# x placed in the output ahead of time, and the last addition of the result made by accumulating stores

## The chip, the cores and the metric

The kernel runs on one core of one Trainium2 chip. The metric is the device time of one execution in microseconds (us). Three runs of the kernel before gave a median of 2445.79 us, from 2444.87 to 2446.43.

## What is computed

For 2048 tokens x of width 1024, all in float32:

```python
xn = _layernorm(x)                                # over the last axis
s  = _A_ref(xn, A_wqkv, A_wo)                     # linear attention, 32 heads, then times wo
h  = _silu(xn @ w1) * (xn @ w3)                   # 3584 wide
g  = _silu(h @ w2)
return x + s * g
```

The change touches the last line: how `x` comes into `x + s * g`.

## The kernel before

Every large product is made with one level of a seven-product scheme (`B11`, `T2`, `T3`, `T1`, `B21`, `T4`, `B22`), each of the seven as three passes over operands that were split into a high and a low part (`split`, L80 to 88; `mm3`, L89 to 93). The split is a cast on ScalarE (ACT, L83) and a subtraction on VectorE (DVE, L84). The program goes through these stages:

1. **Start.** 512 tokens (`xa`) and 512 others (`xb`) are loaded by SyncE's queue (SP), normalised, turned by TensorE (PE, L148) and split. The first four weight tiles (`w0k0_0`, `w0v0_0`, `w0k0_1`, `w0v0_1`, L286) come through the same SP queue, and the first products `ak`, `av` need one of them each. `prepare_rest` forms sums of the tokens on GpSimd (POOL, L190 to 193). The next weights (`wk0_0`, `wv0_0`, L263) go into the two buffers that `xa` leaves, so their loads wait until the last of `xa` has been turned.
2. **Keys, values, queries, gate and up products** for the two halves of the tokens. Intermediates go to memory.
3. **Attention's end** (`s`), which stores s into `s_d`.
4. **The w2 product** in five layers `B0` to `B4` (`layers`), each over the 8 groups of 256 tokens (`NG` = 8, `m` = 0 to 7). A layer loads its left operands (`rA11B` and six others, L890, from `h_d` and `hs_d`), splits them, makes seven products for each group and adds them into the accumulators `acc0` to `acc7`. The additions are by DVE out of PSUM (L846 to L871) and by POOL (L849 to 851).

In the last layer, `B4`, every finished quarter of a group (128 x 512) goes through `finish`: SP loads `ss` (a piece of s) and `xs` (a piece of x); ACT takes the SiLU of the accumulator (L926); DVE multiplies by `ss` (L927) and adds `xs` (L928); POOL issues the store into `out` (L929). That is 32 quarters.

The order of instructions on each engine is not the order of the text: a scheduler with a simulated timeline sets it from dependencies when the program is built. Each engine then works its own list in order. The order of the SP list is the order in which transfers enter SP's queue.

Of the kernel before, what the change touches and what calls it, by code (L numbers as in the profile page):

```python
# [12 lines left out]
ALU = mybir.AluOpType  # L13
# [3 lines left out]
P = 128  # L17
# [5 lines left out]
def tile_linear_attention_times_swiglu(  # L23
# [10 lines left out]
    nc = tc.nc  # L34
    x, out = x[0], out[0]
# [71 lines left out]
    def small(name):  # L107
        return pc.tile([P, C], F32, tag="c", name=name)
# [344 lines left out]
    def half(h):  # L453
# [40 lines left out]
        for pair in range(ND // 2):  # L494
            if h == 0 and pair < 2:
                run(m[2 * pair])
                run(m[2 * pair + 1])
            elif h and pair == 0:
                side_by_side(keys(pair, paired=True), values(pair, paired=True))
            else:  # L500
                run(keys(pair))
                run(values(pair))
            later.extend(uses[pair][2])
# [263 lines left out]
    GT = 2 * P  # L767
    NG = S // GT
# [130 lines left out]
    def hiddens(i, m):  # L899
        h_ = h_d[i][m // NT].rearrange("p (k e) s -> p k e s", e=2)  # L900
        hs = hs_d[i][m // NT]
        return left(m, m % NT, [h_[:, :, e] for e in range(2)], [hs[:, :, e] for e in range(2)],
                    (FB[i][1] - FB[i][0]) // 2, f"B{i}")

    def second_weights(i, n, k):
        t = small(f"r{n}B{i}_{k}")
        nc.sync.dma_start(out=t, in_=second_weight(i, n, k))
        return t
# [9 lines left out]
    def store_s(m, t, n, a):  # L918
        nc.gpsimd.dma_start(out=s_d[2 * m + t][:, n * C:(n + 1) * C], in_=a)  # L919

    def finish(m, t, n, a):
        r0, cols = (2 * m + t) * P, slice(n * C, (n + 1) * C)
        xs, ss = small(f"xs{m}_{t}{n}"), small(f"ss{m}_{t}{n}")
        nc.sync.dma_start(out=ss, in_=s_d[2 * m + t][:, cols])
        nc.sync.dma_start(out=xs, in_=x[r0:r0 + P, cols])
        nc.scalar.activation(a, a, AF.Silu)  # L926
        nc.vector.tensor_mul(a, a, ss)  # L927
        nc.vector.tensor_add(a, a, xs)  # L928
        nc.gpsimd.dma_start(out=out[r0:r0 + P, cols], in_=a)  # L929

    def run(seg, nxt=None, around=None):

        def between(k):
            if m == NG - 1 and nxt:
                if k == 0:
                    nxt.operands(0)
                    for e in range(seg.nk, nxt.nk):
                        nxt.right(e)
                if k < nxt.nk:
                    nxt.right(k)  # L940

        if not seg.X:
            seg.operands(0)
        for m in range(NG):
            if m + 1 < NG:
                seg.operands(m + 1)
            seg.tokens(m, m == 0 or m == NG - 1 and nxt is not None, between)


# [26 lines left out]
    def layer_place(n, i, k):  # L976
# [3 lines left out]
    layers = [Segment(f"B{i}", (f1 - f0) // 2, i == 0, layer_place, lambda n, _, k, i=i: second_weights(i, n, k),  # L980
                      lambda m, i=i: hiddens(i, m), lambda m, t, n: acc[m][:, t, n],
                      finish if i == len(FB) - 1 else None)
              for i, (f0, f1) in enumerate(FB)]
# [2 lines left out]
        layers[0].right(k)  # L986
    acc.extend(pw.tile([P, 2, 2, C], F32, tag=f"acc{m}", name=f"acc{m}") for m in range(NG))
    for i, seg in enumerate(layers):
        run(seg, layers[i + 1] if i + 1 < len(layers) else None)


# [21 lines left out]
```

## Time and profile before

| | before |
|---|---|
| median of three runs | 2445.79 us |
| the profiled execution | 2438.58 us |
| its span in the trace | 2436.8 us |
| mean granted clock of TensorE | 0.992 |
| TensorE busy | 2344.2 us, 96% |
| VectorE busy | 1810.3 us, 74% |
| ScalarE busy | 928.0 us, 38% |
| GpSimd busy | 723.7 us, 30% |
| traffic | 408.62 MB, 168 GB/s |

The profiled execution is one of the kernel's executions, 7.2 us under the median of the three. Busy shares are means over stages that differ: the rows of single stretches tell which engine a stage waits for. A granted clock of 1.00 is 2.4 GHz, and 0.50 is 1.2 GHz.

### The profile page before, as it was taken

Reading aid. Unit: us, or ns where it says so; the run is one execution under the profiler, and the core shown is the slowest. Engines: PE = TensorE matmul, PEld = TensorE weight load, DVE = VectorE, ACT = ScalarE, POOL = GpSimd, SP = SyncE. Lnnn points to the kernel's source line nnn. Section 1 sums busy time; section 2 is a strip of 40 time slices with the busy share of each in tenths; the row PEclk is TensorE's granted clock in tenths of the full one; section 3 lists DMA queues with packets and bytes.
Section 4 is the critical chain, followed back from the end, with each engine's and each line's share of the span. In section 5 each row is a group of like instructions: output and inputs, shape, how many; then the busy total and the mean of one; then the engine's idle time right before and its main releaser. Section 6 shows DMA issues by size and latency. Waiting matters only on the chain.

```text
span 2436.8 us, 30795 instructions
## 1 busy us (share of the span) xinstructions
PE 2344.2 (96%) x10544; PEld 1927.2 (79%) x10544; DVE 1810.3 (74%) x2688; ACT 928.0 (38%) x1663; POOL 723.7 (30%) x909
## 2 busy tenths in 40 slices
PE   6999989999999999999999999999899999999987
PEld 5788777778888888888778888888687887778776
DVE  8645788888887764657888887888655767776797
ACT  4434544332333233445433323333323434343443
POOL 3000021465554310000343543244330032323253
PEclk9999999999999999999999999999999999999999
DMA  4221555665555581124455556457776545454587
GB/s 139 70 69 45 172 168 171 220 212 196 184 203 178 184 290 35 52 83 144 163 192 180 191 191 207 136 187 243 242 234 194 152 130 157 120 163 116 169 288 240
DMA packets 375133, 408.62 MB, mean 168 GB/s; under 512 B 19840, under 2 KB 308608, under 8 KB 374976
## 3 DMA queue, kind: packets, MB, share of 16 engines
q1 hardware_dynamic: 348800, 319.35, 41.9%
q0 software_dynamic: 26176, 87.31, 9.5%
q8 instruction: 82, 1.34, 0.2%
q14 instruction: 75, 0.61, 0.1%
HBM read 268.96 MB, written 137.63 MB: 167 GB/s over the span
## 4 chain that ended last, share of the span: by engine, by line
PE 75%; DVE 11%; DMA 6%; issue 5%; ACT 1%; POOL 1%; SPq 0%; DVEq 0%; POOLq 0%; ACTq 0%
PE dB L93 1%; PE kv L442 1%; PE cB L91 1%; PE dB L91 1%; PE dB L92 1%; PE cB L93 1%; PE cB L92 1%; PE aB L93 1%; PE aB L91 1%; PE aB L92 1%; DMA wpr<-wp_d 1%; PE trk L409 1%; PE trv L409 1%; DMA rA11B<-h_d 1%; PE cs L93 1%
## 5 line engine op out<-in xcount | busy, mean ns | idle before, releaser
L511 POOL DMA_DIRECT2D pq_d<-pq x32 | 17.5, 548 | 501.2 <-DVE pq L403 461.6
L564 POOL DMA_DIRECT2D h_d<-sg x112 | 62.0, 553 | 331.1 <-DVE sg L563 320.6
L849 POOL TENSOR_TENSOR acc<-acc,uB 128x512 f32<-128x512 f32 x25 | 41.9, 1676 | 157.8 <-DVE uB L846 157.8
L546 POOL TENSOR_TENSOR qd<-qd 128x128 f32<-128x128 f32 x32 | 25.4, 795 | 129.1 <-DVE qd L696 121.1
L578 POOL TENSOR_TENSOR w<-w 128x256 f32<-128x256 f32 x28 | 26.4, 944 | 106.7 <-DMA w<-in_B_w 106.5
L826 POOL TENSOR_TENSOR acc<-acc,uB 128x512 f32<-128x512 f32 x7 | 10.9, 1560 | 149.3 <-ACT uB L818 149.3
L410 ACT ACTIVATE kvr<-trk 128x512 f32<-128x512 f32 x32 | 19.1, 597 | 88.0 <-PE trk L409 84.8
L550 POOL TENSOR_TENSOR hs<-sg,hs 128x256 f32<-128x256 f32 x56 | 51.9, 927 | 1.7
L547 POOL TENSOR_TENSOR hs<-hs,sg 128x256 f32<-128x256 f32 x56 | 46.5, 830 | 0.0
L919 POOL DMA_DIRECT2D s_d<-s x32 | 17.5, 546 | 92.9 <-DVE s L856 41.6
L546 POOL TENSOR_TENSOR hs<-sg,sg 128x256 f32<-128x256 f32 x56 | 42.1, 751 | 1.0
L91 PE MATMUL cB<-T,XA22B 128*128 128x512 f32 x87 | 35.0, 403 | 7.3 <-DVE acc L853 7.0
L549 POOL TENSOR_TENSOR hs<-sg 128x256 f32<-128x256 f32 x56 | 41.5, 740 | 0.0
L83 ACT CAST XS4B<-rS4B 128x384 fp32r<-128x384 f32 (+1 forms) x40 | 19.6, 490 | 54.0 <-PE cB L93 44.6
L851 POOL TENSOR_TENSOR acc<-acc,uB 128x512 f32<-128x512 f32 x25 | 40.0, 1600 | 0.0
L84 DVE TENSOR_TENSOR XS1B<-rS1B,XS1B 128x384 fp32r<-128x384 f32 (+1 forms) x40 | 36.4, 910 | 4.1 <-ACT XS1B L83 4.0
L867 DVE TENSOR_TENSOR acc<-cB,acc 128x512 f32<-128x512 f32 x25 | 17.2, 688 | 29.7 <-PE cB L93 29.7
L83 ACT CAST XS1B<-rS1B 128x384 fp32r<-128x384 f32 (+1 forms) x40 | 19.7, 493 | 48.5 <-PE cB L93 26.2
L926 ACT ACTIVATE acc<-acc 128x512 f32<-128x512 f32 x32 | 20.2, 632 | 46.3 <-DVE acc L856 14.1
L83 ACT CAST XA11B<-rA11B 128x384 fp32r<-128x384 f32 (+1 forms) x40 | 19.7, 493 | 44.9 <-PE dB L93 28.4
L83 ACT CAST XS3B<-rS3B 128x384 fp32r<-128x384 f32 (+1 forms) x40 | 19.7, 491 | 43.3 <-DMA rS3B<-hs_d 20.5
L91 PE MATMUL aB<-B,XA12B 128*128 128x512 f32 x87 | 34.1, 392 | 1.9 <-ACT uB L843 1.9
(5861 smaller groups left out, 8899.6 us busy)
## 6 DMA issues: line engine op xcount, KB each, us to landing
h_d<-sg POOLq DMA_DIRECT2D x112, 256.0 KB, 3.1
qs_d<-qd POOLq DMA_DIRECT2D x32, 512.0 KB, 4.1
hs_d<-hs POOLq DMA_DIRECT2D x60, 256.0 KB, 3.5
w<-in_B_w SPq DMA_DIRECT2D x56, 256.0 KB
wt_d<-w SPq DMA_DIRECT2D x28, 512.0 KB
hs_d<-hs SPq DMA_DIRECT2D x52, 256.0 KB
pq_d<-pq POOLq DMA_DIRECT2D x32, 256.0 KB, 3.0
pqd<-pq_d SPq DMA_DIRECT2D x16, 512.0 KB
```

Of the source, the lines that this page charges most:

```text
L83: nc.scalar.copy(out=hi, in_=src)
L91: nc.tensor.matmul(acc, lhsT=wh, rhs=ah, start=start, stop=False, skip_group_check=True)
L92: nc.tensor.matmul(acc, lhsT=wh, rhs=al, start=False, stop=False, skip_group_check=True)
L93: nc.tensor.matmul(acc, lhsT=wl, rhs=ah, start=False, stop=stop, skip_group_check=True)
L409: nc.tensor.transpose(p_[:, t * P:(t + 1) * P], src[:, t * P:(t + 1) * P], ident)
L546: nc.gpsimd.tensor_add(out=s1, in0=a21, in1=a22)
L547: nc.gpsimd.tensor_sub(out=s2, in0=s1, in1=a11)
L549: nc.gpsimd.tensor_sub(out=s3, in0=a11, in1=a21)
L550: nc.gpsimd.tensor_sub(out=s4, in0=a12, in1=s2)
L564: nc.gpsimd.dma_start(out=h_d[i][2 * h + c][:, 2 * k + n], in_=sg[n, c])
L849: G.tensor_add(out=c22, in0=c22, in1=u)
L851: G.tensor_add(out=c12, in0=c12, in1=u)
```

## The change

`finish` no longer loads `xs` and no longer adds it for the groups `m` = 0 to 6. In its place their store into `out` adds to what lies there (`accum_op=ALU.add`). So that x lies there, seven transfers from `x` straight to `out`, of 256 tokens (1 MB) each, are put on SP's queue (`lay_x`). They are written in layer `B1`, ahead of the products of each group. Group 7 stays as before.

```diff
+    ADDED = NG - 1
+
     def finish(m, t, n, a):
         r0, cols = (2 * m + t) * P, slice(n * C, (n + 1) * C)
-        xs, ss = small(f"xs{m}_{t}{n}"), small(f"ss{m}_{t}{n}")
+        ss = small(f"ss{m}_{t}{n}")
         nc.sync.dma_start(out=ss, in_=s_d[2 * m + t][:, cols])
-        nc.sync.dma_start(out=xs, in_=x[r0:r0 + P, cols])
+        if m >= ADDED:
+            xs = small(f"xs{m}_{t}{n}")
+            nc.sync.dma_start(out=xs, in_=x[r0:r0 + P, cols])
         nc.scalar.activation(a, a, AF.Silu)
         nc.vector.tensor_mul(a, a, ss)
-        nc.vector.tensor_add(a, a, xs)
-        nc.gpsimd.dma_start(out=out[r0:r0 + P, cols], in_=a)
+        if m >= ADDED:
+            nc.vector.tensor_add(a, a, xs)
+            nc.gpsimd.dma_start(out=out[r0:r0 + P, cols], in_=a)
+        else:
+            nc.gpsimd.dma_start(out=out[r0:r0 + P, cols], in_=a, accum_op=ALU.add)
+
+    def lay_x(m):
+
+        if m < ADDED:
+            nc.sync.dma_start(out=out[m * GT:(m + 1) * GT, :], in_=x[m * GT:(m + 1) * GT, :])
...
         for m in range(NG):
             if m + 1 < NG:
                 seg.operands(m + 1)
+            if around:
+                around(m)
             seg.tokens(m, m == 0 or m == NG - 1 and nxt is not None, between)
...
-        run(seg, layers[i + 1] if i + 1 < len(layers) else None)
+        run(seg, layers[i + 1] if i + 1 < len(layers) else None, lay_x if i == 1 else None)
```

What the built programs do with it, at three places:

**SP's queue, at the very start of the program** (names: `w0v0_0` and `w0k0_1` are first weight tiles, `out_0` the output, `in_A_x` x):

```order
 L174 DMA xb1_426<-in_A_x 128x1024
 L174 DMA xb2_456<-in_A_x 128x1024
+L942 DMA out_0<-in_A_x 16x16384 x7
 L286 DMA w0v0_0__355<-in_A_wqkv 128x8x128
 L286 DMA w0k0_1__378<-in_A_wqkv 128x8x128
```

The seven transfers wait for no data, and the scheduler has placed all of them here, before the second weight tile and some 2000 us ahead of layer `B1`.

**DVE, the same stretch of the start, as it stands in the changed program** (`xb` are the second 512 tokens; the L84 rows with `w0v0_0`, `w0k0_1` and `w0v0_1` split the weight tiles; `xb3` is the last of the tokens):

```order
L141 TENSOR_SCALAR xb0_424<-xb0_424,mom_213 128x1024
L141 TENSOR_SCALAR xb1_426<-xb1_426,mom_213 128x1024
L403 SCALAR_TENSOR_TENSOR pk0_0_0_500,z_501<-ak0_0__341,pk0_0_0_500 128x512
L421 SCALAR_TENSOR_TENSOR zacc_74<-z_501,zacc_74 128x1
L84 TENSOR_TENSOR B11v0_0__357<-w0v0_0__355,B11v0_0__357 128x512
L84 TENSOR_TENSOR B21v0_0__360<-w0v0_0__355,B21v0_0__360 128x512
L84 TENSOR_TENSOR B11k0_1__380<-w0k0_1__378,B11k0_1__380 128x512
L84 TENSOR_TENSOR B21k0_1__383<-w0k0_1__378,B21k0_1__383 128x512
L84 TENSOR_TENSOR B11v0_1__403<-w0v0_1__401,B11v0_1__403 128x512
L84 TENSOR_TENSOR B21v0_1__406<-w0v0_1__401,B21v0_1__406 128x512
L130 BN_STATS bs_460<-xb3_458 128x6 x2
```

Before, the splits of the weight tiles stood between those of the first tokens; now they stand behind the normalising of `xb0` and `xb1`, and with them everything that follows in this list.

**POOL, in the last layer, as it stands in the changed program** (L849 to 851 add to the accumulators, L937 is the accumulating store):

```order
L849 TENSOR_TENSOR acc4_15109<-acc4_15109,uB4_4_19574 128x512
L850 TENSOR_TENSOR acc4_15109<-acc4_15109,uB4_4_19574 128x512
L851 TENSOR_TENSOR acc4_15109<-acc4_15109,uB4_4_19574 128x512
L937 DMA out_0<-acc4_15109 128x512 x4
L849 TENSOR_TENSOR acc5_15110<-acc5_15110,uB4_5_19707 128x512
```

Before, the last of the four stores of a group stood behind the three additions of the next group; now all four stand ahead of them.

## Rows read from the trace of the kernel before

**Rows 1.** The page: busy time and share of each engine.

```profile
PE 2344.2 (96%) x10544; PEld 1927.2 (79%) x10544; DVE 1810.3 (74%) x2688; ACT 928.0 (38%) x1663; POOL 723.7 (30%) x909
```

**Rows 2.** Busy time by stretch, last layer; at the end clock, DMA share, GB/s.

```profile
2300.00:2314.40 14.40, 12.54 (x53) 9.39 (x52) 13.87 (x19) 5.42 (x11) 6.73 (x5) 1.00 0.76 238
2314.40:2328.80 14.40, 12.85 (x57) 10.33 (x56) 14.05 (x22) 6.79 (x14) 7.12 (x5) 1.00 0.62 184
2328.80:2343.20 14.40, 12.42 (x53) 9.63 (x53) 13.21 (x17) 4.51 (x9) 11.48 (x11) 1.00 0.92 294
2343.20:2357.60 14.40, 12.93 (x57) 10.38 (x56) 14.13 (x26) 6.48 (x13) 3.04 (x7) 1.00 0.99 327
2357.60:2372.00 14.40, 13.29 (x59) 10.68 (x58) 12.58 (x21) 6.13 (x12) 6.91 (x7) 1.00 0.96 312
2372.00:2386.40 14.40, 14.27 (x63) 11.49 (x62) 13.83 (x22) 6.07 (x12) 6.91 (x7) 1.00 0.93 301
```

**Rows 3.** Groups of DVE instructions in the last layer: busy us, mean ns.

```profile
L928 DVE TENSOR_TENSOR acc<-acc,xs 128x512 f32<-128x512 f32 x30 | 25.3, 843 | 0.0
```

**Rows 4.** DMA queues and issues from 2300 us on: packets, MB, share; us to landing.

```profile
q0 software_dynamic: 2560, 8.39, 16.0%
...
out<-acc POOLq DMA_DIRECT2D x32, 256.0 KB, 4.2
```

**Rows 5.** Timeline of SP's queue, first 62 us: start, us, what was issued.

```profile
0.74 1.81 SPq L120 DMA_DIRECT2D xa<-in_A_x  x4
...
5.72 0.45 SPq L286 DMA_DIRECT2D w0v__355<-in_A_wqkv  x1
...
17.69 0.37 SPq L286 DMA_DIRECT2D w0v__401<-in_A_wqkv  x1
...
44.86 0.37 SPq L263 DMA_DIRECT2D wk__692<-in_A_wqkv  x1
```

**Rows 6.** Busy time by stretch, the first 15 us (columns as in rows 2).

```profile
0.00:5.00 5.00, 0.00 (x0) 0.00 (x0) 2.31 (x14) 1.28 (x1) 0.70 (x6) 1.00 0.61 211
5.00:10.00 5.00, 0.00 (x0) 0.00 (x0) 4.97 (x18) 0.41 (x2) 0.00 (x0) 1.00 1.06 375
10.00:15.00 5.00, 2.20 (x8) 1.43 (x8) 5.00 (x22) 2.56 (x6) 0.00 (x0) 1.00 1.07 368
```

**Rows 7.** DMA traffic of the first 100 us in 40 slices of 2.5 us.

```profile
GB/s 61 362 409 342 410 325 189 108 105 0 182 34 0 0 0 0 0 0 163 257 3 0 10 326 90 36 358 25 0 101 318 0 21 339 66 0 0 0 0 0
```

**Rows 8.** Timeline of ACT at the start: the casts that waited for weight tiles.

```profile
15.72 0.62 ACT L83 CAST B11v__357<-w0v__355 128x512 fp32r<-128x512 f32 x1 [0.77 <-DMA w0v__355<-in_A_wqkv]
...
21.54 0.62 ACT L83 CAST B11v__403<-w0v__401 128x512 fp32r<-128x512 f32 x1 [0.47 <-DMA w0v__401<-in_A_wqkv]
```

**Rows 9.** Timeline of PE at the start.

```profile
36.73 0.66 PE L148 MATMUL tS<-ident,xa 128*128 128x128 f32 x4 [1.09 <-POOL xa L192]
...
38.88 0.47 PE L91 MATMUL ak__387<-A,B21k__383 128*128 128x512 f32 x1
...
57.43 0.50 PE L91 MATMUL bk__713<-S,T2k__699 128*128 128x512 f32 x1 [1.35 <-ACT T2k__699 L83]
```

**Rows 10.** Timeline of DVE at the start: the landing of wk0_0, and two splits.

```profile
50.09 0.73 DVE L282 TENSOR_TENSOR wk__692<-wk__692 128x512 f32<-128x512 f32 x1 [2.73 <-DMA wk__692<-in_A_wqkv]
...
52.42 1.27 DVE L84 TENSOR_TENSOR S<-tS,S 128x512 fp32r<-128x512 f32 x2
```

**Rows 11.** Timeline of POOL at the start: first and last of eight sums of tokens.

```profile
43.66 1.28 POOL L190 TENSOR_TENSOR S1x<-xb 128x512 f32<-128x512 f32 x1
...
53.70 1.28 POOL L193 TENSOR_TENSOR xa<-xa 128x512 f32<-128x512 f32 x1
```

**Rows 12.** Busy time by stretch behind the last product (columns as in rows 2).

```profile
2423.00:2424.00 1.00, 0.08 (x1) 0.00 (x0) 1.00 (x3) 0.20 (x1) 0.21 (x1) 1.00 0.38 125
...
2427.00:2428.00 1.00, 0.00 (x0) 0.00 (x0) 0.83 (x2) 0.00 (x0) 0.19 (x1) 0.83 0.28 106
2428.00:2429.00 1.00, 0.00 (x0) 0.00 (x0) 0.00 (x0) 0.00 (x0) 0.54 (x1) 0.50 0.41 156
```

## The prediction

> **What bounds the kernel now.** I read the page first, then stretches of the two ends that the change touches, then single engines in them. TensorE is busy for 96% of the span [rows 1]; so a gain can come only where it idles, and a new idle time of TensorE is paid in full unless something later had slack. The last layer is such a place. A group of tokens is 63 matmuls, 14.27 us where nothing is missing; in the five stretches ahead of that one TensorE did 12.54, 12.85, 12.42, 12.93 and 13.29 us of work in 14.4 us, while VectorE was busy for 12.6 to 14.1 us [rows 2]. There VectorE is as full as TensorE, and the DMA engines are close to full too, 0.92 to 0.99 in the later stretches. The start is the other place: TensorE waits for weight tiles, which come through SP's one queue in the order of issue [rows 5, 8].
>
> **Part 1: the additions go.** 28 of the 32 additions of `xs` leave VectorE. They took 843 ns on average [rows 3], so 28 x 0.843 = 23.6 us, or 3.4 us for each group. VectorE falls from about 13.8 to 10.4 us in a stretch, below TensorE's 14.27. What TensorE lost in the five stretches against 14.27 us is 1.73 + 1.42 + 1.85 + 1.34 + 0.98 = 7.3 us [rows 2]; more than that can't be won, since from there on it is full. What is late next is the operand loads, as the DMA engines stay near 0.95. I take 5 us, with 0 and 7.3 as ends.
>
> **Part 2: xs loads go, plain stores become accumulating ones.** In a group 1 MB of x is no longer loaded, and the store of 1 MB must now also read what it adds to. No row shows an accumulating store. Plain stores moved 8.39 MB in 16.0% of 137 us, 21.9 us [rows 4], which is 0.68 us for 256 KB. From below, an accumulating store costs 0.68 us like a plain one, and the layer gets 28 x 0.68 = 19 us of DMA time back, which hides what is left. From above, I take three passes of that size (read, read, write), 2.05 us, against 1.37 us for store and load before: 28 x 0.68 = 19 us more DMA time in a layer whose six stretches [rows 2] average 0.86; those have 0.14 x 14.4 = 2 us free each, and seven groups would swallow some 4 us in stretches that are already full and then pay: up to 15 us. I take the middle, two passes, which equals the store and the load that it replaces: nothing. POOL's order changes too: the fourth store of a group now stands ahead of the next group's additions. It waits for a SiLU and a multiply after the group's last product, some 3 us, and the additions behind it can't begin before two products of the next group, 2/7 x 14.27 = 4.1 us, are done. So that costs nothing; if the cover goes, the next additions are late, then the product into that bank.
>
> **Part 3: seven transfers from x to out.** They are written in layer B1, but the built order has them behind `xb2` and ahead of `w0v0_0`, so in the first 10 us. That is what decides. Ahead of them in the queue are eight transfers of 512 KB (`xa` four, `w0k0_0`, `xb` three), 4.19 MB. The traffic was 211, 375 and 368 GB/s in the first three stretches of 5 us [rows 6]: 1.06 + 1.88 MB by 10 us, the other 1.25 MB 3.4 us later, at 13.4 us. Then come 7 x 1.049 = 7.34 MB from memory to memory. No row has such a transfer. From below: each byte counts once, at the fastest slice of the start, 410 GB/s [rows 7]: 17.9 us. From above: each byte loads the memory twice, read and written, at 368 GB/s: 14.68 / 0.368 = 39.9 us. I take twice at 410 GB/s, 35.8 us: both ends of the transfer lie in the same memory, unlike in any transfer of the rows. The Trainium skill ("DMA: Bandwidth & Descriptors", section on latency and other measured facts) has copies from memory to memory with long rows at 207 to 214 GB/s; by it 7.34 MB would be an estimated 34.3 us and the whole sum below 1.5 us less. No row here shows it.
>
> `w0v0_0` then lands at T = 13.4 + 35.8 + 1.4 (its own 0.52 MB) = 50.6 us; before it was there at 15.72 [rows 8]. What follows, by durations of before:
>
> - Its split frees a buffer 2.0 us after landing (15.72 to 17.69 [rows 5, 8]), `w0v0_1` is issued, and lands 3.85 us later (17.69 to 21.54): T + 5.9. Cast and subtraction take 1.3 us: T + 7.2.
> - From there TensorE's list has, ahead of the load of `wk0_0`, 36 matmuls of 0.2265 us (14.27 / 63 [rows 2]) and 40 transposes at 2.15 us for twenty (36.73 to 38.88 [rows 9]): 8.15 + 4.3 = 12.5 us: T + 19.6.
> - `wk0_0` takes 5.2 us from issue to use (44.86 [rows 5] to 50.09 [rows 10]): T + 24.9.
> - From its landing to the first product with it were 7.3 us (50.09 to 57.43 [rows 9, 10]); in the new DVE list four more splits of 0.6 us [rows 10] lie between: 9.7 us, T + 34.6 = 85.2 us.
>
> The sums of tokens on POOL are no longer than this: `xb3` lands about T + 7, is ready at about T + 11.5, and the eight operations take 11.3 us (43.66 to 54.98 [rows 11]), T + 22.8, ahead of the load above. The first such product came at 57.43 us [rows 9]. **The start is later by 85.2 - 57.4 = 27.8 us**, all of it idle time of TensorE, and nothing later gives it back. With the copy's two ends it is 9.9 and 31.9 us.
>
> TensorE idles from about 24.5 us (24 matmuls after 19 us) to T + 1.3. Behind the last product of the program the granted clock fell from 1.00 to 0.83 and then 0.50, which is 1.2 GHz, some 4 us after the last work [rows 12]. So the 24 matmuls behind the idle time may run at half the clock: 0 to 24 x 0.2265 = 5.4 us more, less 0.5 us in which they would have waited for `w0v0_1` anyway. I take 1 us.
>
> **Sum.** 27.8 + 1 - 5 = +23.8 us, so +24. The profiled execution took 2438.6 us; with +24 it would be 2462.6. It lies 7.2 us (0.3%) under the median of the runs, 2445.8; on that, **2470 us**.
>
> **The rivals.**
>
> - *The copies are fast.* Each byte counts once: the start loses 9.9 us, the last layer gives 5 back: +5, 2451 us. For it: the engines moved 410 GB/s when one end was this same memory. Against: reads and writes of the same memory at once are in no row.
> - *The copies hold nothing up (faster).* If the transfers behind them in the queue overtake them, `w0v0_0` keeps its time, the start costs nothing and the last layer's 5 to 7 us remain: -6, 2440 us. It decides where the weight tile comes before 27 us: T - 22.8 is the loss, so a loss of 5 us is T = 27.8, a copy of 13 us or 565 GB/s, more than any row has. So it takes an overtaking, and before, the weight tiles were used in the order of issue [rows 5, 8]. The Trainium skill (same page, section on queues, rings and completion order) has each engine take a queue's descriptors in order, which by the same reckoning is the loss above; the two casts in rows 8 agree.
> - *The accumulating stores become the bound.* Three passes: the last layer loses 15 us where I gave it 5: 27.8 + 1 + 15 = +44, 2490 us. For it: DMA shares of 0.92 to 0.99 [rows 2] and a landing of 4.2 us already for plain stores [rows 4]. Against: the loads of xs are gone.
>
> That the change doesn't do what its text says is not a rival but part 3: the place of the transfers is the built order's.
>
> **How the numbers follow.** A measurement of this kernel can tell about 0.2%, 5 us, from no change. My forecast, with copies of 25 to 40 us, has a chance of 0.62; its own range is 2458 to 2483. Fast copies have 0.17 (half of it within 5 us, a little of it faster), slow stores 0.12, no hold-up 0.09. Slower: 0.62 + 0.12 + 0.09 = 0.83; same: 0.08; faster: 0.09. From the range I leave out the fastest cases and the slowest: 2449 to 2485 us.
>
> **What would show it.** In the changed profile SP should issue seven `out<-in_A_x` before 14 us, the cast of `w0v0_0` should start near 51 us, TensorE should be idle from 24.5 to 52 us with a granted clock below 1.00 at the end of it, and the first product with `wk0_0` should come near 85 us. In the last layer L928 should be there 4 times, VectorE below 11 us and TensorE near 14.2 us in a stretch of 14.4. I am wrong if the cast of `w0v0_0` starts before 30 us, if TensorE's idle time at the start grows by less than 10 us, or if the stretches of the last layer get longer with DMA shares of 1.

## The result, and the profile after

The changed kernel took 2455.9 us (median of five runs, 2455.37 to 2458.33) against 2445.79 us before (2442.68 to 2449.47): a ratio of 1.0047, 95% interval 1.0036 to 1.0058. It is 10.1 us slower. The prediction said slower, by 24 us: the direction and the place were right, the size was less than half of what was forecast. The profiled execution took 2455.37 us, its span is 2453.6 us.

SP's queue in the changed kernel, from its timeline (start, us, what was issued; compare [rows 5]):

```profile
5.86 7.35 SPq L942 DMA_DIRECT2D out<-in_A_x  x7
13.96 0.39 SPq L286 DMA_DIRECT2D w0v__355<-in_A_wqkv  x1
16.72 5.45 SPq L286 DMA_DIRECT2D w0k__378<-in_A_wqkv  x1
22.61 12.77 SPq L286 DMA_DIRECT2D w0v__401<-in_A_wqkv  x1
...
59.21 0.37 SPq L263 DMA_DIRECT2D wk__692<-in_A_wqkv  x1
```

The seven copies stand where the prediction had them, ahead of `w0v0_0`, and all of them were issued by 13.2 us. `wk0_0` is fetched 14.35 us later than before (59.21 against 44.86). The casts that wait for the weight tiles, from ACT's timeline (compare [rows 8]):

```profile
38.32 0.62 ACT L83 CAST B11v__357<-w0v__355 128x512 fp32r<-128x512 f32 x1 [9.46 <-DMA w0v__355<-in_A_wqkv]
...
41.69 0.62 ACT L83 CAST B11v__403<-w0v__401 128x512 fp32r<-128x512 f32 x1 [0.47 <-DMA w0v__401<-in_A_wqkv]
```

`w0v0_0` is there at 38.3 us, 22.6 us later than before, but 12.3 us earlier than the 50.6 us of the prediction. What TensorE waits for over the whole program shows where this lands (engine and line, releaser: us in total, times, longest):

```profile
PE av__364 L91 <- ACT B11v__357 L83: 12.7, 1, 12.7
PE tA L148 <- DVE v L132: 11.2, 1, 11.2
PE cB L91 <- DVE acc L853: 7.3, 6, 2.9
PE bk__713 L91 <- ACT T2k__699 L83: 6.5, 1, 6.5
```

The first row is new, and the fourth stood at 1.35 us before [rows 9]: 12.7 + 6.5 = 19.2 us of idle time in two waits, both downstream of that weight tile. A wait of the kernel before, for the sums of tokens on POOL, is gone in exchange:

```profile
PE tS L148 <- POOL xa L192: 5.3, 4, 3.5
```

So TensorE's idle time at the start has grown by 19.2 - 1.35 - 5.3 = 12.5 us. On TensorE's own timeline the two waits end at these instructions (compare [rows 9], where the second began at 57.43, so it is 15.6 us later now):

```profile
38.99 0.79 PE L91 MATMUL av__364<-A,B11v__357 128*128 128x512 f32 x1 [12.71 <-ACT B11v__357 L83]
...
73.00 0.80 PE L91 MATMUL bk__713<-S,T2k__699 128*128 128x512 f32 x1 [6.51 <-ACT T2k__699 L83]
```

Busy time by stretch at the start (stretch, its length, PE, PEld, DVE, ACT, POOL, granted clock, DMA share, GB/s; compare [rows 6]):

```profile
10.00:15.00 5.00, 2.20 (x8) 1.43 (x8) 5.00 (x22) 2.51 (x6) 0.00 (x0) 1.00 1.13 467
15.00:20.00 5.00, 4.86 (x26) 4.82 (x27) 4.01 (x7) 2.90 (x6) 0.00 (x0) 1.00 1.19 421
20.00:25.00 5.00, 4.33 (x20) 3.23 (x19) 5.00 (x11) 1.10 (x3) 0.00 (x0) 1.00 1.18 406
25.00:30.00 5.00, 1.28 (x6) 0.74 (x4) 3.56 (x13) 2.71 (x4) 2.66 (x2) 0.92 0.68 223
30.00:35.00 5.00, 0.00 (x0) 0.00 (x0) 0.37 (x1) 0.00 (x0) 4.76 (x5) 0.50 0.81 237
35.00:40.00 5.00, 1.01 (x2) 0.79 (x3) 1.03 (x2) 1.14 (x2) 3.12 (x3) 0.50 1.07 267
```

These rows count the bytes of a piece (a packet of one DMA engine) in the stretch in which it starts. A copy is 16 pieces of 64 KB that start close together, so a stretch of 5 us holds either one copy or two, and 406 and 421 GB/s are no rates. In slices of 0.675 us, from 13 to 40 us, the starts of the seven copies stand apart, some 3 us each:

```profile
GB/s 1529 0 0 1068 485 0 0 97 1469 0 0 0 1262 291 0 0 680 777 97 0 97 1068 388 0 0 291 1165 97 0 0 8 109 143 188 255 335 323 297 285 236
```

Over all of the copies, as one stretch (columns as above):

```profile
12.90:34.80 21.90, 11.58 (x52) 9.50 (x52) 15.04 (x37) 7.31 (x13) 7.23 (x6) 0.87 1.00 345
```

So the copies took some 22 us, with all engines busy (DMA share 1.00), at 345 GB/s counted once (7.34 of the 7.56 MB in this row are theirs). That is somewhat below the 410 GB/s of the fastest loads in [rows 7], and far from half of it; of a memory that is loaded twice nothing shows here. The three weight tiles move behind them, from 34 us on. In the last three of the 5 us rows TensorE runs dry, and its granted clock falls from 1.00 to 0.50 (1.2 GHz).

The last layer, in stretches of one group as in [rows 2]:

```profile
2314.00:2328.40 14.40, 12.45 (x54) 9.70 (x53) 12.96 (x18) 8.31 (x17) 7.72 (x5) 1.00 0.80 248
2328.40:2342.80 14.40, 12.81 (x56) 9.95 (x55) 14.16 (x22) 6.11 (x13) 5.30 (x4) 1.00 0.60 161
2342.80:2357.20 14.40, 11.47 (x44) 8.92 (x43) 13.23 (x18) 5.34 (x12) 9.83 (x9) 0.88 1.05 227
2357.20:2371.60 14.40, 14.40 (x66) 11.91 (x64) 9.64 (x17) 6.20 (x13) 7.77 (x8) 1.00 1.06 253
2371.60:2386.00 14.40, 14.40 (x64) 11.70 (x63) 12.31 (x16) 5.63 (x12) 6.70 (x7) 1.00 0.97 233
```

The later stretches are what the prediction wanted: VectorE falls to 9.6 to 12.3 us, TensorE is full. The first two are as before. The third is worse than any before: 11.47 us of work at a mean clock of 0.88, after a wait of 2.9 us for VectorE (`cB` for the addition of L853, the longest in the third row of the waits above).

The accumulating stores, by DMA queue and issue from 2314 us on, and POOL's group (compare [rows 4]):

```profile
q0 software_dynamic: 4352, 8.39, 34.7%
...
out<-acc POOLq DMA_DIRECT2D x32, 256.0 KB, 6.1
```

```profile
L937 POOL DMA_DIRECT2D out<-acc x28 | 24.3, 878 | 45.6 <-DVE acc L932 45.6
```

The stores' queue took 34.7% of 139.6 us, 48.4 us; less four plain stores at 0.68 us [rows 4] that is 45.7 / 28 = 1.63 us for an accumulating store of 256 KB, 2.4 times a plain one. It lands 6.1 us after its issue (4.2 before).

### The profile page after: what moved, and what is told of

The parts are those of the page before. It is cut to its first block, busy times and chain, and to the rows that moved or that the text cites. A ratio compares the mean times of both kernels' runs of the same rounds, so it can differ in the third digit from the quotient of the medians.

```text
span 2453.6 us, 30661 instructions
## 1 busy us (share of the span) xinstructions
PE 2350.7 (96%) x10544; PEld 1935.0 (79%) x10544; DVE 1792.6 (73%) x2660; ACT 932.1 (38%) x1665; POOL 723.8 (29%) x909
## 4 chain that ended last, share of the span: by engine, by line
PE 65%; DVE 6%; DMA 5%; issue 2%; ACT 1%; POOL 0%; SPq 0%; POOLq 0%; DVEq 0%; ACTq 0%
PE cB L91 1%; PE cB L93 1%; PE dB L93 1%; PE dB L91 1%; PE dB L92 1%; PE cB L92 1%; PE aB L93 1%; PE aB L91 1%; PE aB L92 1%; DMA wpr<-wp_d 1%; DMA rS1B<-hs_d 1%; PE bB L93 1%; PE bB L91 1%; PE bB L92 1%; PE den L664 1%
## 5 line engine op out<-in xcount | busy, mean ns | idle before, releaser
L511 POOL DMA_DIRECT2D pq_d<-pq x32 | 17.4, 545 | 510.5 <-DVE pq L403 471.4
L849 POOL TENSOR_TENSOR acc<-acc,uB 128x512 f32<-128x512 f32 x25 | 39.0, 1558 | 153.5 <-DVE uB L846 153.5
L919 POOL DMA_DIRECT2D s_d<-s x32 | 17.4, 544 | 94.3 <-DVE s L856 34.3
L84 DVE TENSOR_TENSOR XS1B<-rS1B,XS1B 128x384 fp32r<-128x384 f32 (+1 forms) x40 | 36.7, 917 | 7.9 <-ACT XS1B L83 7.9
L83 ACT CAST XS4B<-rS4B 128x384 fp32r<-128x384 f32 (+1 forms) x40 | 19.6, 490 | 53.5 <-PE cB L93 44.5
L937 POOL DMA_DIRECT2D out<-acc x28 | 24.3, 878 | 45.6 <-DVE acc L932 45.6
L442 PEld LDWEIGHTS kv<-kvr 128*128 128x128 f32 x256 | 34.4, 195 | 2.6
```

The source lines that it names most:

```text
L83: nc.scalar.copy(out=hi, in_=src)
L84: return nc.vector.tensor_sub(out=lo, in0=src, in1=hi.bitcast(F32))
L849: G.tensor_add(out=c22, in0=c22, in1=u)
```

## The experiments

Two theories at first. **Queue**: the loss is the start's, because the copies stand ahead of the weight tiles; the last layer gains. **Stores**: the accumulating stores eat the gain or more. All ratios are to runs of the kernel before on the same chip.

**The kernel before, once more.** No edit; it shows how far one profiled execution may differ from another.

> The kernel before once more, for its trace. Its first profiled execution (2438.6 us) lay 7 us below the median of its runs. If this one is near 2446 us, its trace shows in which stretch those 7 us lie; both theories say that it isn't the first 60 us, as TensorE's first product with wk0_0 should again come at 57 us.

Measured: 2444.97 us, span 2443.2 us, against 2436.8 us of the span that the prediction rests on. Stretches of this execution, and then of the first one:

```profile
60.00:90.00 30.00, 26.62 (x115) 21.57 (x113) 23.45 (x42) 10.31 (x19) 0.00 (x0) 0.94 0.38 119
```

```profile
60.00:90.00 30.00, 29.54 (x135) 24.20 (x134) 23.53 (x45) 11.69 (x20) 0.00 (x0) 1.00 0.35 113
```

In the first profiled execution the clock stayed at 1.00 through the idle times of the start; here it fell to a mean of 0.94. The first store of the line L511 comes at 243.9 us here and came at 237.7 us there, so 6.2 of the 6.4 us between the two spans are lost by then. Of these 1.7 us are lost by the first product with `wk0_0` (59.13 us against 57.43), which the expectation had excluded. Another 2.9 us are a longer wait a little later, ahead of the product `bv__823` (0.5 us in the first execution):

```profile
PE bv__823 L91 <- ACT T2v__809 L83: 3.4, 1, 3.4
```

The mark of L511 is at 243.0 and 242.5 us in the next two kernels that leave the start alone. So the trace of [rows 5 to 11] shows a start that was 5 to 6 us better than in these three executions.

**The copies held until layer B1.** The accumulating stores stay.

```diff
-            nc.sync.dma_start(out=t, in_=where[n])
+            loaded.append(nc.sync.dma_start(out=t, in_=where[n]))
...
-            nc.sync.dma_start(out=out[m * GT:(m + 1) * GT, :], in_=x[m * GT:(m + 1) * GT, :])
+            with tc.issue_after(loaded[-1].ins):
+                nc.sync.dma_start(out=out[m * GT:(m + 1) * GT, :], in_=x[m * GT:(m + 1) * GT, :])
```

> The seven transfers from x to out are held on SP's queue until layer B1, each behind the operand loads of its group, where the text of the change has them; the accumulating stores stay. Theory 'queue': the loss comes from the transfers standing ahead of the weight tiles at the start, so w0v0_0 is used near 15.7 us again, the first product with wk0_0 comes near 57.4 us, and the time is 1 to 2 us below that of the kernel before (what the last layer gained in the trace): 2443 to 2446 us. Theory 'stores': the accumulating stores in the last layer carry the loss, and the time stays near 2453 to 2456 us.

Measured: 2441.8 us, ratio 0.9985 (0.9977 to 0.9994). The whole loss is gone, and 3.4 us of the last layer's gain are left. Moving the issue of the copies from 6 us to 1962 us and later is worth 10.1 + 3.4 = 13.5 us.

**The copies alone**, at the start; the additions and plain stores as before.

```diff
-        if m >= ADDED:
-            xs = small(f"xs{m}_{t}{n}")
-            nc.sync.dma_start(out=xs, in_=x[r0:r0 + P, cols])
+        xs = small(f"xs{m}_{t}{n}")
+        nc.sync.dma_start(out=xs, in_=x[r0:r0 + P, cols])
...
-        if m >= ADDED:
-            nc.vector.tensor_add(a, a, xs)
-            nc.gpsimd.dma_start(out=out[r0:r0 + P, cols], in_=a)
-        else:
-            nc.gpsimd.dma_start(out=out[r0:r0 + P, cols], in_=a, accum_op=ALU.add)
+        nc.vector.tensor_add(a, a, xs)
+        nc.gpsimd.dma_start(out=out[r0:r0 + P, cols], in_=a)
```

> The seven transfers stay at the start, and the last layer is as before (xs loaded, added by VectorE, plain stores that write over what was laid there). Theory 'queue': all of the loss stays and the small gain of the last layer goes: 2456 to 2459 us, with w0v0_0 used near 38 us. Theory 'stores': near 2446 us.

Measured: 2457.97 us, ratio 1.0051 (1.0039 to 1.0063), +12.8 us. The two halves add up: +12.8 for the copies, -3.4 for the finish, +9.4 together, where the change has +10.1 (each within some 3 us). The theory of the stores falls.

**No x at all for seven groups**: the kernel before without the loads of `xs` and the additions there, with plain stores.

```diff
-        xs, ss = small(f"xs{m}_{t}{n}"), small(f"ss{m}_{t}{n}")
+        ss = small(f"ss{m}_{t}{n}")
...
-        nc.sync.dma_start(out=xs, in_=x[r0:r0 + P, cols])
+        if m >= NG - 1:
+            xs = small(f"xs{m}_{t}{n}")
+            nc.sync.dma_start(out=xs, in_=x[r0:r0 + P, cols])
...
-        nc.vector.tensor_add(a, a, xs)
+        if m >= NG - 1:
+            nc.vector.tensor_add(a, a, xs)
```

> The kernel before without x in the result for the groups 0 to 6: no load of xs, no addition, plain stores (the output there is s times g). It is the most that the last layer could give if the additions and the loads cost nothing elsewhere. Theory 'queue' with VectorE as what bounds the last layer: 5 to 7 us under the kernel before, 2439 to 2441 us. If the last layer is bound by something else (landing of operands), under 2 us: 2444 to 2446 us.

Measured: 2440.81 us, ratio 0.9982 (0.9973 to 0.9990). So 4.4 us is all that the last layer gives when x costs neither DMA time nor VectorE time; the accumulating stores take about 1 us of it, which these intervals can't separate from nothing. Its third stretch has the same hole as the changed kernel's, though its DMA engines are well below full:

```profile
2332.80:2347.20 14.40, 11.47 (x44) 8.96 (x43) 13.62 (x19) 5.85 (x12) 7.73 (x9) 0.88 0.85 261
```

TensorE waits there for VectorE (2.9 us, for L853's addition), as in the changed kernel. So neither accumulating stores nor full DMA engines are needed for that hole. It came with the additions of `xs` gone; that the order of VectorE's other instructions changed with them, and makes the hole, is likely and was not shown.

**Three copies at the start, four in layer B1.** The edit is that of the held copies, for `m >= 3` only.

> Three of the seven copies stay at the start, four are held until layer B1; the finish is the changed kernel's. In the changed kernel the packets of the seven copies ended near 31.8 us and the cast of w0v0_0 began at 38.3 us. Theory 'fixed part': a copy is 18.4 / 7 = 2.6 us, and the weight tile behind the copies needs 6.5 us however many they are: cast at 13.4 + 7.9 + 6.5 = 27.8 us, first product with wk0_0 34.7 us later at 62.5 (58 to 59 in kernels without copies at the start), so some 3.5 us of the 3.4 us that the last layer gives are spent: about 2445 us. Theory 'all in the copies': (38.3 - 13.4 - 1.4) / 7 = 3.4 us for each, cast at 24.9, first such product at 59.6, about 2442.5 us.

Measured: 2445.48 us, ratio 1.0003 (0.9993 to 1.0013). The cast of `w0v0_0`:

```profile
24.33 0.62 ACT L83 CAST B11v__357<-w0v__355 128x512 fp32r<-128x512 f32 x1 [0.21 <-DMA w0v__355<-in_A_wqkv]
```

It came at 24.3 us, as "all in the copies" had it (24.9): four more copies cost 38.3 - 24.3 = 14.0 us, 3.5 us for each MB. The first product with `wk0_0` began at 62.52 us and the time is that of the other theory, so here 38.2 us lie between the two and not 34.7. Some 2 us of that lie ahead of the fetch of `wk0_0` (issued at 47.18 us, 22.9 us after the cast; 20.9 in the changed kernel). Behind the fetch TensorE waits for the sums of tokens on POOL again, as before the change and unlike in the changed kernel:

```profile
56.20 1.11 PE L148 MATMUL tS<-ident,xa 128*128 128x128 f32 x4 [3.90 <-POOL xa L192]
```

So with the tile this early another chain has a part in the time of that product; how much of the 3.5 us is its doing stays open.

**One copy behind each weight piece.** All seven copies early, but from 60 us on, each behind a weight piece of layer s.

```diff
+        pieces.append(fetched[0])
...
-            nc.sync.dma_start(out=out[m * GT:(m + 1) * GT, :], in_=x[m * GT:(m + 1) * GT, :])
+            with tc.issue_after(pieces[m + 1].ins):
+                nc.sync.dma_start(out=out[m * GT:(m + 1) * GT, :], in_=x[m * GT:(m + 1) * GT, :])
```

> Same queue, same large pieces, the accumulating stores kept; the seven copies stand one behind each of the second to eighth weight pieces of layer s (from about 55 us on) instead of ahead of w0v0_0. Theory 'place' (a copy costs only where the first product of the next step waits for the tile behind it): each copy delays the next weight piece by 3.5 us, the pieces are fetched some 10 us apart and wait in their buffer, so nothing is lost: 2442 us, like the kernel with the copies in layer B1. Rival 'anywhere early': the pieces behind the copies have no slack, up to 7 x 3.5 = 24 us are lost at the start and the last layer gives 3 back: up to 2466 us.

Measured: 2442.15 us, ratio 0.9989 (0.9980 to 0.9998). As cheap as in layer B1. The stretch that takes three of the copies has the same work as in the kernel before (its row for 60 to 90 us stands above), at almost twice the traffic:

```profile
60.00:90.00 30.00, 26.57 (x113) 21.50 (x113) 23.43 (x43) 10.30 (x19) 0.00 (x0) 0.94 0.62 222
```

It isn't the early traffic that costs, but that it stands ahead of a tile for which TensorE has no other work.

**The copies on ACT's queue**, behind the casts of the first weight tile.

```diff
...
-            nc.sync.dma_start(out=out[m * GT:(m + 1) * GT, :], in_=x[m * GT:(m + 1) * GT, :])
+            with tc.issue_after(weight_casts[1].ins):
+                nc.scalar.dma_start(out=out[m * GT:(m + 1) * GT, :], in_=x[m * GT:(m + 1) * GT, :])
```

> The seven copies move to ACT's DMA queue, behind the casts of the first weight tile (some 12 us), so they move at the same time as in the changed kernel; SP's queue holds only loads. Theory 'queue' (the loss is the place behind the copies in SP's queue): w0v0_0 is cast before 20 us, the two weight tiles after it come slower while the copies last but before 32 us, and the start loses 0 to 4 us: 2442 to 2446 us. Theory 'traffic' (14.7 MB moved in the first 35 us hold the loads up wherever they are queued): the cast of w0v0_0 or of w0v0_1 comes after 33 us, and the time is 2452 to 2458 us.

Measured: 2464.34 us, ratio 1.0080 (1.0060 to 1.0099): worse than in SP's queue, and worse than either theory said. SP's queue and ACT's first cast of `w0v0_0`:

```profile
5.75 0.45 SPq L291 DMA_DIRECT2D w0v__355<-in_A_wqkv  x1
37.54 0.38 SPq L291 DMA_DIRECT2D w0k__378<-in_A_wqkv  x1
```

```profile
37.55 0.62 ACT L85 CAST B11v__357<-w0v__355 128x512 fp32r<-128x512 f32 x1 [22.57 <-DMA w0v__355<-in_A_wqkv]
```

The tile was issued at 5.75 us, 4.3 us ahead of the first copy, on a queue without copies, and landed at 37.5 us all the same. By queue (q10 is ACT's, q1 SP's), from 15 to 25 us (packets, MB, share):

```profile
q10 hardware_dynamic: 96, 3.15, 89.7%
q1 hardware_dynamic: 96, 0.05, 1.7%
```

The copies took nearly all of the traffic; SP's queue got 0.05 MB in these 10 us. The loss is larger than in SP's queue. ACT's order, too, was made for an early tile: its cast stands there ahead of six casts of `A` for the first products, ACT sat idle for 22.57 us in front of it, and TensorE waited 19.57 us for those casts:

```profile
39.71 0.79 PE L93 MATMUL ak__341<-A,B11k__334 128*128 128x512 f32 x1 [19.57 <-ACT A L85]
```

In the changed kernel these first products ran ahead of the long wait. The theory that the place in SP's queue is the cause falls in this form: the tile waits for the copies on either queue. The Trainium skill ("DMA: Bandwidth & Descriptors", section on issuing engines that are not separate DMA queues) says that transfers of all queues run on the same 16 engines and interleave; the two rows agree, and show how unequal the shares may be.

**The copies in pieces of 512 bytes**, in the changed kernel's place. A copy of the changed kernel is 16 pieces of 64 KB.

```diff
-            nc.sync.dma_start(out=out[m * GT:(m + 1) * GT, :], in_=x[m * GT:(m + 1) * GT, :])
+            r0 = m * GT
+            nc.sync.dma_start(out=out[r0:r0 + GT, :].rearrange("r (h c) -> h r c", c=C // 4),
+                              in_=x[r0:r0 + GT, :].rearrange("r (h c) -> h r c", c=C // 4))
```

> The same seven copies in the same place, but each cut into pieces of 512 bytes instead of 64 KB. If a copy is limited by pieces as the loads of the weight tiles are (pieces of 512 bytes, 290 GB/s in the kernel before): 7.34 / 0.29 = 25.3 us, and the weight tile behind them comes without the slow start that it had behind the large pieces: cast of w0v0_0 at 13.4 + 25.3 + 2 = 41 us, some 3 us more than the changed kernel: 2459 us. If the 6.5 us behind the copies are a price of the change from copies to loads, not of large pieces: cast at 45 us, 2463 us. If small pieces load the memory twice: cast above 60 us, 2480 us.

Measured: 2474.67 us, ratio 1.0119 (1.0092 to 1.0146). The cast came at 58.14 us, between the second expectation and the third, and the traffic was flat:

```profile
20.00:45.00 25.00, 6.13 (x27) 4.45 (x26) 8.99 (x22) 4.28 (x7) 10.55 (x8) 0.70 0.57 174
```

By its rate alone it looked like the doubled load of the prediction after all. The next run showed another reading.

**Pieces of 2 KB**: the same edit with `c=C`, so the view is 2 x 256 x 512 instead of 8 x 256 x 128.

> The same seven copies in the changed kernel's place, cut into pieces of 2 KB. Pieces of 64 KB kept w0v0_0 back by (38.3 - 13.4) = 24.9 us for 7.34 MB, 295 GB/s; pieces of 512 bytes moved at 174 GB/s. If a piece has a fixed part and a part by its bytes (on each of 16 engines 47 ns for 512 bytes, 3.6 us for 64 KB: 20 ns and 0.054 ns for a byte), 2 KB take 131 ns, 250 GB/s: 29 us for the copies, cast of w0v0_0 near 44 us, 2461 us. If all but large pieces load the memory twice (174 GB/s): cast near 58 us, 2475 us. If 2 KB are as good as 64 KB: 38 us, 2456 us.

Measured: 2575.2 us in one execution, 130 us slower than before, outside every expectation. Its traffic:

```profile
40.00:120.00 80.00, 0.00 (x0) 0.00 (x0) 0.00 (x0) 0.00 (x0) 0.00 (x0) 0.50 0.13 51
```

A DMA share of 0.13 is 2 of 16 engines (0.125), and the 0.57 of the run before is near 8 of 16. The outermost dimension of the view was 2 and 8. So these two runs didn't compare pieces but numbers of engines: 51 / 2 = 25.5 GB/s for each engine, 174 / 8 = 21.8. The Trainium skill (the same page, section on why a DMA increments its semaphore by 16) ties the number of engines to the slowest dimension of the view, and the shares of 0.13 and 0.57 agree. Two runs with 1792 rows outermost put it to the test.

**512 bytes on all engines**: eight transfers of 1792 x 128.

```diff
-        if m < ADDED:
-            nc.sync.dma_start(out=out[m * GT:(m + 1) * GT, :], in_=x[m * GT:(m + 1) * GT, :])
+        if m == 0:
+            for c0 in range(0, D, 128):
+                nc.sync.dma_start(out=out[:ADDED * GT, c0:c0 + 128], in_=x[:ADDED * GT, c0:c0 + 128])
```

> The same bytes in the same place in pieces of 512 bytes, as eight transfers of 1792 rows (one for each block of 128 columns) instead of seven whose outermost of three dimensions was 8. Theory 'engines' (a transfer is dealt out over the DMA engines by its outermost dimension, so the kernel with 8 x 256 x 128 used half of them, the one with 2 x 256 x 512 two): 174 GB/s / 8 = 21.8 GB/s for each engine, 348 GB/s on 16: 21 us for the copies, cast of w0v_0 at 13.4 + 21.1 + 2 = 36.5 us, 2454 us. Theory 'pieces' (512 bytes are slow in a copy): 174 GB/s again, cast at 58 us, 2474 us.

Measured: 2459.81 us, ratio 1.0067 (1.0052 to 1.0082).

```profile
13.00:36.00 23.00, 11.29 (x52) 9.18 (x52) 15.12 (x37) 7.21 (x12) 8.47 (x7) 0.84 1.08 300
```

**2 KB on all engines**: the same with 512 columns, two transfers.

> The same bytes in the same place in pieces of 2 KB, as two transfers of 1792 rows. Theory 'engines': 51 GB/s / 2 = 25.5 GB/s for each engine, 408 GB/s on 16: 18 us, cast of w0v_0 at 13.4 + 18 + 2 = 33.4 us, 5 us ahead of the changed kernel's: 2451 us. Theory 'pieces' (2 KB slower than 512 bytes, as 51 GB/s stood against 174): cast after 100 us, over 2500 us.

Measured: 2456.65 us, ratio 1.0054 (1.0039 to 1.0069).

```profile
13.00:36.00 23.00, 11.95 (x52) 9.84 (x52) 15.01 (x37) 7.34 (x12) 8.03 (x6) 0.87 1.05 323
```

The theory of the engines holds: with all of them (DMA shares 1.08 and 1.05) the same pieces move at 300 and 323 GB/s instead of 174 and 51. They are slower than it reckoned (348 and 408), so 16 engines do less than 16 times what one does in those two runs; what takes the rest no run shows. The casts of `w0v0_0` came at 41.1 and 40.0 us, later than expected (36.5, 33.4) and close to the 38.3 us of large pieces, whose 345 GB/s are not far above.

**512 bytes on ACT's queue**: the eight transfers, placed as in the run on ACT's queue above.

> The copies on ACT's queue behind the first casts, as before, but in pieces of 512 bytes (eight transfers of 1792 rows). If each engine takes turns between its queues piece by piece, the weight tile (pieces of 512 bytes) now loses one piece's time to each of its own instead of 3.5 us to 64 KB: w0v_0 lands within 4 us of its old time, cast before 22 us, the next two tiles by 30 us, 2443 to 2448 us. If a load just stands behind all copies that were started before it, or the memory is what is short: cast near 37 us as with 64 KB, 2456 to 2464 us.

Measured: 2464.93 us, ratio 1.0089 (1.0072 to 1.0106), no better. SP's queue now moved eight times the bytes in the same 10 us, from 15 to 25:

```profile
q10 hardware_dynamic: 5413, 2.75, 97.1%
q1 hardware_dynamic: 796, 0.40, 15.1%
```

That is 0.40 MB against 0.05 beside pieces of 64 KB, but it isn't the same tile. From 13 to 17 us, and then from 17 to 22 us:

```profile
q1 hardware_dynamic: 1084, 0.65, 57.7%
q10 hardware_dynamic: 1315, 0.67, 56.9%
```

```profile
q10 hardware_dynamic: 3294, 1.67, 115.1%
```

`w0v0_0` is 1024 pieces (0.52 MB). They had all started by 17 us, since SP's queue moved nothing in the next 5 us; beside pieces of 64 KB the tile landed at 37.5. Most of the 0.40 MB belong to the next tile, which was issued at 18.64 us and had no piece moved before 22 us. But the cast of `w0v0_0` came late for a new reason, on ACT itself:

```profile
18.33 11.12 ACTq L949 DMA_DIRECT2D out<-in_A_x  x3
29.52 5.19 ACTq L949 DMA_DIRECT2D out<-in_A_x  x2
34.76 0.62 ACT L85 CAST B11v__357<-w0v__355 128x512 fp32r<-128x512 f32 x1 [4.67 <-issue]
```

ACT spent 16 us in issuing five of its transfers, and no cast could pass them. So the cast at 34.8 us tells nothing of when the tile landed. The tile came through early beside small pieces, as the theory of turns has it, but the next tile's wait of 3 us behind them does not fit equal turns; in what turns the engines serve two queues is not shown.

## Why the prediction came out as it did

**The place (part 3): right.** Seven copies by 13.2 us, `w0v0_0` behind them, TensorE idle from 26.3 us. That it is these copies, and their place, the kernels with the copies alone (+12.8 us) and with the copies late (-3.4 us) show. The built order of the engines' lists changed together with the place, and no run holds one of the two while it changes the other; what the order alone costs or gives here is not shown.

**The copy's price (part 3): wrong, and this is the step that failed.** "I take twice at 410 GB/s, 35.8 us: both ends of the transfer lie in the same memory." The copies moved at 345 GB/s counted once and took 21.9 us (12.9 to 34.8 us), so the term was 14 us too large. The tile behind them took 3.5 us instead of 1.4. Together they took 38.3 - 13.4 = 24.9 us, against 35.8 + 1.4 = 37.2. The lower end, 17.9 + 1.4 = 19.3, was nearer: it lacked 4 us for the copies, which did not reach 410 GB/s, and 2 for the tile. The Trainium skill's 207 to 214 GB/s for copies ("DMA: Bandwidth & Descriptors", section on latency and other measured facts), which gave an estimated 34.3 us, does not hold for these: the row of 345 GB/s decides. The rival of the fast copies was the better description, and its chance of 0.17 too small. That no row showed such a copy was a reason for a wide choice, not for the slow half of it.

**The chain behind the tile: right in sum.** T + 34.6 was predicted from the first use of the tile to the first product with `wk0_0`; 73.00 - 38.32 = 34.7 us were measured. That the two agree so closely is in part luck. `w0v0_1` came at T + 3.4 (41.69 - 38.32) and not at T + 5.9, while the fetch of `wk0_0` came at T + 20.9 and not at T + 19.6, and 2.0 us of these 20.9 are the low clock of the next paragraph, which the prediction had outside the chain.

**The low clock: undersized, and partly there before.** One us was allowed. After the first idle time nine matmuls ran at 0.43 us (38.99 to 42.95, 4.0 us instead of 2.0), and after the second the same:

```profile
73.00:77.00 4.00, 4.00 (x9) 3.15 (x10) 3.31 (x6) 2.01 (x4) 0.00 (x0) 0.50 0.02 4
```

That is 3.9 us, 2.0 in the chain and 1.9 behind it.

**The median: a loss counted twice.** In its second profiled execution the kernel before lost some 6 us in the same part of the program, partly at the low clock and partly in waits, and the two kernels that leave the start alone lost some 5; the execution that was profiled first did not. The start of the changed kernel, which is 17.7 us later than in that profile at the first store of L511 (255.4 against 237.7), is 11.5 us later than in the second (243.9). Adding the change to the median of the runs counted those 6 us twice: once in the median, once as a new loss.

The sum for the start: 27.8 us were predicted at the first product with `wk0_0`; less 12.3 for the tile's landing and plus 0.1 for the chain, these are the 15.6 us measured there. Behind it 2.1 us were lost, where 1 was allowed: 17.7. Less 6.2 us for what the kernel before loses itself, the start is 11.5 us later, against 12.8 in the medians.

**The additions (part 1): right in sign, oversized.** 5 us were taken, of at most 7.3. VectorE fell as said (9.6 to 12.3 us in the later stretches), and TensorE filled them (14.40). With x free of any cost the layer gives 4.4 us; 3.4 are left with accumulating stores, 2.7 beside early copies (12.8 - 10.1), which the intervals can't tell apart. The wait of 2.9 us in the third stretch is a new one, which the prediction had not looked for.

**The stores (part 2): a middle that held.** Two passes, 1.37 us, were taken; 1.63 us were measured, inside 0.68 to 2.05. The 28 of them cost about 1 us of time, if anything, and the rival in which the stores become the bound is refuted: the held copies with accumulating stores run faster than the kernel before.

**The range** held: 2455.9 lies in 2449 to 2485, at its lower end, nearer to the 2451 of the fast copies than to the 2470 of the forecast.

## What to carry to other kernels

A transfer that nothing in the program waits for still belongs somewhere: read where the built order puts it, and give it a place where no tile behind it is waited for. Here the same seven copies cost 12.8 us ahead of the first weight tiles. Behind the later weight pieces they cost no more than in layer B1, as far as the intervals can tell (ratios 0.9989 and 0.9985), and another queue doesn't take them out of the way. In such a place the change gains a little: 2441.8 us with the copies held until layer B1 beats the kernel before by 0.15%, and the changed one by 13.5 us.

Before adding a loss to a median, ask whether the median already contains it: look at the granted clock in the idle times of the profiled execution, and at a second execution if there is one.

## What was not expected of the hardware

- A view with a small outermost dimension leaves most DMA engines idle: 2 x 256 x 512 moved 51 GB/s at a DMA share of 0.13, 8 x 256 x 128 174 GB/s at 0.57, 1792 x 512 323 GB/s at 1.05. The seven copies in the first view cost 130 us.
- Seven copies from memory to memory, in pieces of 64 KB, moved at 345 GB/s counted once: nearer to the loads (410 GB/s at their fastest) than to half of them.
- A load in pieces of 512 bytes beside copies in pieces of 64 KB on another queue got 0.05 of 3.2 MB in 10 us and landed at 37.5 us; beside copies in pieces of 512 bytes all of its pieces had started by 17 us.
- An engine that issues copies of many small pieces is held by the issuing: five of them kept ACT for 16 us; seven of 64 KB pieces had taken SP 7.4 us in all.
- An accumulating store of 256 KB takes 1.63 us of the DMA engines against 0.68 for a plain one, 878 ns to issue on POOL against 546, and lands in 6.1 us against 4.2.
